# Two-layer sliding attention and feed-forward on one core: second products of a chunk's last group listed ahead of the next chunk's first ones, and weight forms made by ScalarE and GpSimd, six pairs per chunk

## The chip, the cores and the metric

The kernel runs on 1 core of one Trainium2 chip. The metric is the device time of one launch in microseconds (us), and the figure of a kernel is the median of its runs. Engines are named as in the profile: PE is TensorE, DVE is VectorE, ACT is ScalarE, POOL is GpSimd, SP is SyncE, which here only issues transfers.

## The reference

Two kinds of layer alternate, twice each, on 2048 rows of 576 numbers. The weights are shared between the two rounds.

```python
def _A_ref(x, wqkv, wo):                      # 32 heads of 18
    q, k, v = split(x @ wqkv)
    idx = pos[:, None] - 2 * arange(8)        # each row sees 8 rows, 2 apart, itself and back
    logits = (q . k[idx]) * 18 ** -0.5        # rows before the start are masked
    return (softmax(logits) . v[idx]) @ wo

def _B_ref(x, w1, w2):                        # 576 -> 4608 -> 576
    return silu(x @ w1) @ w2

x = x + _A_ref(layernorm(x), wqkv, wo)
x = x + _B_ref(layernorm(x), w1, w2)
x = x + _A_ref(layernorm(x), wqkv, wo)
x = x + _B_ref(layernorm(x), w1, w2)
```

All matrix products are made of float16 halves (a high and a low part of each operand, three products of halves in place of one), so that float32 accuracy is kept.

## The kernel before

**Chunks.** The rows are cut into 4 chunks of 512 (4 tiles of 128). With two rounds there are 8 chunk steps, s = 0 to 7; steps 0 to 3 are the first round, 4 to 7 the second. Chunk step s runs LayerNorm, the q/k/v products, attention on DVE, the projection by wo, LayerNorm, and the feed-forward. The attention part of step s+1 is worked on while PE does the feed-forward of step s, so PE nearly always has a product to make.

**Feed-forward.** Steps 0 and 1 use plain products (`ffn`). Steps 2 to 6 use `ffn_pairs`: the first products (w1) go by 18 pairs of 128-column blocks, each pair made by seven products P1 to P7 (a Strassen-Winograd scheme) of 7 matmuls each (line 1176). ACT copies partial sums out of PSUM (L1180), DVE adds to them (L1183), ACT applies silu (L1199, L1201, L1203), ACT makes the high half of h (L1206) and DVE the low half (L1209). The pairs form six groups of three. The second products of a group (w2, in `second`, line 1334) take h of its three pairs for each of four tiles j, 36 matmuls per tile, 144 per group; DVE adds the result into x (L894). Step 7 uses `ffn_twice`, whose second products follow a Strassen scheme too (lines 1237 and 1307).

**Forms.** Before the first products of a chunk, `forms` makes seven combinations of x on DVE (L1127, L1132), halves them on ACT (L1141, L1142) and DVE (L1146, L1147), and SP turns them by transposing transfers (L1151) into tile xb, which the matmuls of L1176 read. Nine such places exist, and a chunk holds seven, so most forms of a chunk are turned only as the last pair of the chunk ahead frees places.

**Weight forms.** Step 7 needs combinations of the w2 blocks. `prepare_second` makes them for 18 pairs q: SP loads two blocks (L1081, L1082), POOL makes four subtractions (L1088), ACT the high half with a scale (L1090), DVE the low half (L1092), POOL stores the result to DRAM (L1094, tile wts). Before, nine pairs are made after the attention of step 6 and nine after that of step 7, in two places of the area `kvs`, which the attention's keys and values use too; so the first two units of step 7's attention have a `hold` on `("wts", 8)`.

**Order.** Nothing is scheduled at run time. Each operation is declared with an engine, a planned duration and a priority (`op`), and a planner (`Plan.order`) writes one fixed instruction list per engine: at each moment of its own plan the ready operation of lowest priority number goes next. An operation that is late on the chip makes everything behind it on its engine wait. In step s the first products of pair q have priority s + 0.5 + 0.01 q; the q/k/v products, the attention and the projection of step s+1 have s, so they go first wherever they are ready. The second products of groups 0 to 4 have s + 0.5 + 0.01 (g+1) 3 and a little; those of the last group have s + 0.5 + SEAM with SEAM = 1, which is the priority of the next chunk's first products. "Seam" below means the stretch from the last pair of one chunk to the first pairs of the next.

Of the kernel before, what the change touches and what calls it, by code (L numbers as in the profile page):

```python
# [269 lines left out]
def sliding_attention_silu_ffn(ctx: ExitStack, tc: tile.TileContext, x, wqkv, wo, w1, w2, out):  # L270
# [230 lines left out]
    highs = []  # L501
    attended = []
    turned = []
# [237 lines left out]
    def attention(s, xT, wq, more=None):  # L741
# [4 lines left out]
        for u in range(NU):  # L746
# [12 lines left out]
            else:  # L759
                w = wq(u)  # L760
                hold = {S3: [("wts", NP // 2 - 1)], S3 + 1: [("wts", NP - 1)]}.get(s, []) if u < 2 else []
                if blk == 0:
                    def clear(kv=kv):
                        nc.gpsimd.memset(T(kv)[0:2, 0:3], 0.0)
                        nc.gpsimd.memset(T(kv)[0:1, 3:7], 0.0)
                    op("POOL", 1.86, clear, hold, [(kv, "edge")], pr_, after=free)
                else:
                    def edge(kv=kv, u=u):
                        a, b = T(kv)[0:2, 0:3], T(kv)[0:1, 3:7]
                        e = eds[lay, par, u]  # L770
# [298 lines left out]
    def prepare_second(q, prio, after):  # L1069

        b = Buf("v2")

        def rows6():
            return T(b)[:, 0:12 * KH].bitcast(F32).rearrange("p (a b) -> p a b", a=6)

        def split():
            return T(b)[:, 12 * KH:].rearrange("p (a b c) -> p a b c", a=4, b=2)

        def load():
            t = rows6()  # L1080
            nc.sync.dma_start(t[:, 0:2, :], w2[2 * q * P:(2 * q + 1) * P, :].rearrange("p (h c) -> p h c", h=2))  # L1081
            nc.sync.dma_start(t[:, 2:6:3, :], w2[(2 * q + 1) * P:(2 * q + 2) * P, :].rearrange("p (h c) -> p h c", h=2))  # L1082
        op("SP", 0.8, load, ["wsc"], [(b, 0)], prio, nbytes=P * 4 * KH * 4, after=after, lanes=2)

        def sums():
            t = rows6()
            for r, x, y in ((3, 1, 0), (1, 5, 1), (4, 5, 3), (2, 2, 4)):
                nc.gpsimd.tensor_tensor(t[:, r], t[:, x], t[:, y], op=ALU.subtract)  # L1088
        op("POOL", 3.4, sums, [(b, 0)], [(b, 0)], prio)
        op("ACT", 1.2, lambda: nc.scalar.activation(split()[:, :, 0, :], rows6()[:, 1:5], AF.Copy, scale=wst[:, q:q + 1]),  # L1090
           [(b, 0), "wsc"], [(b, 1)], prio)
        op("DVE", 1.4, lambda: nc.vector.scalar_tensor_tensor(split()[:, :, 1, :], rows6()[:, 1:5], wst[:, q:q + 1], split()[:, :, 0, :],  # L1092
                                                              op0=ALU.mult, op1=ALU.subtract), [(b, 0), (b, 1)], [(b, 1)], prio)
# [226 lines left out]
    def second(s, g, ng, hb, wbs, xs, d2):  # L1320
# [217 lines left out]
```

## Time and profile before

| what | value |
|---|---|
| runs of the kernel before | 2146.66, 2148.25, 2164.3 us; median 2148.25 us |
| profiled execution, its own time | 2152.83 us |
| its span, first to last instruction | 2151.0 us |
| PE busy in the span | 2106.6 us (98%) |
| DVE, ACT, POOL busy | 1709.5, 1010.5, 493.4 us |
| mean granted TensorE clock | 0.997 of full speed |

The profile shows one execution. Busy time of PE is the union of its matmuls, so span less busy time is the time in which no matmul ran. A window row gives for a stretch of the span the busy time and count of each engine, the granted TensorE clock (PEclk) and the share of the transfer engines. A wait row names the waiting engine, tile and line, then what released it, the total, the number of times and the longest. A chain row tells what the last-ending work hung on at that time.

### The profile page before, as it was taken

Reading aid. Unit: us, or ns where it says so; the run is one execution under the profiler, and the core shown is the slowest. Engines: PE = TensorE matmul, PEld = TensorE weight load, DVE = VectorE, ACT = ScalarE, POOL = GpSimd, SP = SyncE. Lnnn points to the kernel's source line nnn. Section 1 sums busy time; section 2 is a strip of 40 time slices with the busy share of each in tenths; the row PEclk is TensorE's granted clock in tenths of the full one; section 3 lists DMA queues with packets and bytes.
Section 4 is the critical chain, followed back from the end, with each engine's and each line's share of the span. In section 5 each row is a group of like instructions: output and inputs, shape, how many; then the busy total and the mean of one; then the engine's idle time right before and its main releaser. Section 6 shows DMA issues by size and latency. Waiting matters only on the chain.

```text
span 2151.0 us, 41793 instructions
## 1 busy us (share of the span) xinstructions
PE 2106.6 (98%) x16125; PEld 1567.9 (73%) x16125; DVE 1709.5 (79%) x2657; ACT 1010.5 (47%) x1839; POOL 493.4 (23%) x747
## 2 busy tenths in 40 slices
PE   8999999999999999999999999999999999999999
PEld 4556566655667888777886788867878867887887
DVE  8999999999978999689944999349995369964544
ACT  7555788654344553444243443344434434344443
POOL 2224656243332330011000100011031100233322
PEclk9999999999999999999999999999999999999999
DMA  6476777697889988875767667676688956679773
GB/s 181 153 227 248 248 262 262 168 281 244 227 198 291 325 256 219 197 215 162 185 173 181 200 194 181 155 192 205 202 245 216 279 148 184 182 232 281 235 209 114
DMA packets 360015, 460.16 MB, mean 214 GB/s; under 512 B 148216, under 2 KB 286820, under 8 KB 355848
## 3 DMA queue, kind: packets, MB, share of 16 engines
q1 hardware_dynamic: 316904, 316.49, 53.4%
q0 software_dynamic: 40896, 139.89, 20.3%
q8 instruction: 126, 2.06, 0.4%
q10 hardware_dynamic: 2016, 1.11, 0.2%
q14 instruction: 73, 0.60, 0.1%
HBM read 330.61 MB, written 78.29 MB: 190 GB/s over the span
## 4 chain that ended last, share of the span: by engine, by line
PE 81%; DMA 8%; DVE 6%; issue 2%; ACT 1%; POOL 1%; SPq 0%; ACTq 0%; DVEq 0%; POOLq 0%
PE acc L1334 22%; PE z L1176 11%; PE misc L1176 10%; PE z L710 8%; PE z L1376 6%; PE acc L1395 6%; PE misc L710 5%; PE acc L887 4%; PE acc L1307 4%; PE z L1237 2%; PE misc L1237 2%; DMA xb<-yh 2%; DMA w<-w2s 1%; DMA w<-wfs 1%; DMA wq<-in_B_w_dram 1%
## 5 line engine op out<-in xcount | busy, mean ns | idle before, releaser
L1334 PE MATMUL acc<-w,h 128*128 128x288 f16 x4320 | 558.0, 287 | 1.2 <-DVE x L894 1.2
L1334 PEld LDWEIGHTS <-h 128*128 128x128 f16 x4320 | 423.6, 98 | 105.3 <-issue 1.4
L1176 PEld LDWEIGHTS <-w 128*128 128x128 f16 x4410 | 432.4, 98 | 76.7 <-issue 15.9
L1176 PE MATMUL z<-xb,w 128*128 128x256 f16 x2261 | 289.2, 274 | 8.2 <-DMA xb<-yo 4.0
L1176 PE MATMUL misc<-xb,w 128*128 128x256 f16 x2149 | 275.2, 273 | 8.1 <-ACT wq L1180 4.3
L1395 PE MATMUL acc<-w,h 128*128 128x288 f16 x1728 | 215.6, 286 | 2.1 <-DMA w<-w2s 2.1
L710 PEld LDWEIGHTS <-xa 128*128 128x128 f16 x1344 | 131.0, 98 | 112.7 <-issue 2.1
L1395 PEld LDWEIGHTS <-h 128*128 128x128 f16 x1728 | 168.4, 98 | 46.5 <-issue 2.5
L894 DVE SCALAR_TENSOR_TENSOR x<-acc,d,x 128x576 f32<-128x576 f32 x160 | 129.4, 811 | 83.2 <-PE acc L1334 77.4
L846 DVE TENSOR_TENSOR prs<-kvs,pe 128x1152 f32<-128x1152 f32 x128 | 169.6, 1351 | 0.8
L813 DVE TENSOR_TENSOR prs<-qts,kvs 128x2304 f32<-128x2304 f32 x64 | 163.3, 2552 | 5.3 <-ACT qts L781 4.1
L817 DVE TENSOR_REDUCE lg<-prs 128x128 f32<-128x2304 f32 x64 | 163.0, 2547 | 1.0
L853 DVE TENSOR_TENSOR prs<-prs 128x1152 f32<-128x1152 f32 (+1 forms) x128 | 135.1, 1056 | 3.3
L793 POOL DMA_DIRECT2D kvs<-kvs x64 | 33.9, 537 | 448.4 <-ACT qts L781 423.2
L1376 PE MATMUL z<-xb,w 128*128 128x512 f16 x588 | 130.8, 383 | 5.1 <-ACT h L1378 1.9
L887 PE MATMUL acc<-wo,yo 128*128 128x288 f16 x896 | 113.4, 286 | 1.7 <-ACT yo L489 1.2
L710 PE MATMUL z<-wq,xa 128*128 128x432 f16 x602 | 114.7, 346 | 0.0
L710 PE MATMUL misc<-wq,xa 128*128 128x432 f16 x574 | 110.3, 346 | 2.7 <-ACT xa L489 1.3
L1376 PEld LDWEIGHTS <-w 128*128 128x128 f16 x588 | 57.8, 99 | 75.5 <-issue 4.3
L1088 POOL TENSOR_TENSOR kvs<-kvs 128x288 f32<-128x288 f32 x72 | 67.0, 941 | 180.5 <-DMA kvs<-in_B_w_dram 124.3
L887 PEld LDWEIGHTS <-yo 128*128 128x128 f16 x896 | 87.6, 98 | 25.0 <-ACT yo L489 1.4
L1237 PEld LDWEIGHTS <-w 128*128 128x128 f16 x882 | 86.1, 98 | 15.8 <-issue 2.7
(286 smaller groups left out, 3193.0 us busy)
## 6 DMA issues: line engine op xcount, KB each, us to landing
w<-wfs SPq DMA_DIRECT2D x756, 160.0 KB
w<-w2s SPq DMA_DIRECT2D x216, 288.0 KB
wq<-wqs SPq DMA_DIRECT2D x17, 1080.0 KB
kvs<-kd POOLq DMA_DIRECT2D x8, 1584.0 KB, 10.3
w<-w1s SPq DMA_DIRECT2D x36, 320.0 KB
wfs<-xa POOLq DMA_DIRECT2D x18, 640.0 KB, 4.6
w2s<-w POOLq DMA_DIRECT2D x36, 288.0 KB, 4.1
kvs<-in_B_w_dram SPq DMA_DIRECT2D x36, 288.0 KB
```

The lines of the kernel that those rows point to most:

```text
L710: nc.tensor.matmul(T(m)[:, :3 * UC], a, b, start=n == 0, stop=n == len(pl) - 1)
L813: nc.vector.tensor_tensor(T(pr), T(qt)[:, j:j + 2, None, :].to_broadcast([P, 2, W, UC]), win(T(kv), j, 2), op=ALU.mult)
L817: nc.vector.tensor_reduce(T(lg)[:, j:j + 2].rearrange("p a w h -> p (a w h)"), T(pr).rearrange("p a w (h d) -> p (a w h) d", d=DH), axis=A ...
L846: nc.vector.tensor_tensor(T(pr)[:, a].rearrange("p w (h d) -> p w h d", d=DH), v, T(pe)[:, j + a, :, :, None].to_broadcast([P, W, UH, DH]) ...
L853: nc.vector.tensor_tensor(t[:, :, 0:h, :], t[:, :, 0:h, :], t[:, :, h:2 * h, :], op=ALU.add)
L887: nc.tensor.matmul(T(acc)[:, h, 0:288], a, b[:, h * 288:(h + 1) * 288], start=n == 0, stop=n == len(pl) - 1)
L894: nc.vector.scalar_tensor_tensor(t, T(acc)[:, :, 0:288], d, t, op0=ALU.mult, op1=ALU.add)
L1176: nc.tensor.matmul(t, w[:, u, :], v[:, r, :], start=first and m == 0, stop=m == 6, skip_group_check=True)
L1237: nc.tensor.matmul(t, w[:, u, :], v[:, r, :], start=first and m == 0, stop=m == 6, skip_group_check=True)
L1334: nc.tensor.matmul(T(acc)[:, h, 0:288], T(hb[t])[:, a, f, j * P:(j + 1) * P], T(wbs[t][f])[:, h, w, :], start=t == 0 and f == 0 and m == 0 ...
L1376: nc.tensor.matmul(T(z), v, u, start=m == 0, stop=m == len(pl) - 1)
L1395: nc.tensor.matmul(T(acc)[:, h, 0:288], T(hb[q])[:, a, j * P:(j + 1) * P], T(wbs[q][0])[:, h, w, :], start=q == 0 and m == 0, stop=q == n ...
```

## The change

- `second`: with LATE = 8 the second products of the last group get s + 0.5 + 0.18 and a little, as the other groups do, in every step that uses `second` (2 to 6). The number of matmuls stays.
- `prepare_second`: ACT scales the two loaded blocks in place (L1089 of the changed kernel), POOL makes the four subtractions (L1094), ACT the high half (L1096), POOL the low half by one subtraction of 1152 numbers per partition (L1097), POOL stores (L1099). DVE has no part in it. The forms are in one place of area `xa` (16 KH, where the turned input of the q/k/v products stands too) in place of two of `kvs`.
- Six pairs each are declared after the last q/k/v product of steps 4, 5 and 6 (list `fed`). The `hold` of step 7 is gone.
- `load_wt` reads the products 5, 7, 4, 6 from the places in their new sequence.

```diff
+LATE = 8
+FORMS = {4: (0, 6), 5: (6, 12), 6: (12, 18)}
-    parts("v2", [(KV, 0), (KV, 10 * WB)], [20 * KH], F16)
+    part("v2", XA, 1, [16 * KH], F16)
-                hold = {S3: [("wts", NP // 2 - 1)], S3 + 1: [("wts", NP - 1)]}.get(s, []) if u < 2 else []
...
+                    if u == NU - 1 and j == NJ - 1:
+                        fed.append(done)
...
         def load():
-            t = rows6()
-            nc.sync.dma_start(t[:, 0:2, :], w2[2 * q * P:(2 * q + 1) * P, :].rearrange("p (h c) -> p h c", h=2))
-            nc.sync.dma_start(t[:, 2:6:3, :], w2[(2 * q + 1) * P:(2 * q + 2) * P, :].rearrange("p (h c) -> p h c", h=2))
+            for f in range(2):
+                nc.sync.dma_start(rows4()[:, f * D:(f + 1) * D], w2[(2 * q + f) * P:(2 * q + f + 1) * P, :])
         op("SP", 0.8, load, ["wsc"], [(b, 0)], prio, nbytes=P * 4 * KH * 4, after=after, lanes=2)
+        op("ACT", 1.2, lambda: nc.scalar.activation(rows4(), rows4(), AF.Copy, scale=wst[:, q:q + 1]), [(b, 0), "wsc"], [(b, 0)], prio)
         def sums():
-            for r, x, y in ((3, 1, 0), (1, 5, 1), (4, 5, 3), (2, 2, 4)):
+            for r, x, y in ((0, 1, 0), (1, 3, 1), (3, 3, 0), (2, 2, 3)):
                 nc.gpsimd.tensor_tensor(t[:, r], t[:, x], t[:, y], op=ALU.subtract)
-        op("POOL", 3.4, sums, [(b, 0)], [(b, 0)], prio)
-        op("ACT", 1.2, lambda: nc.scalar.activation(split()[:, :, 0, :], rows6()[:, 1:5], AF.Copy, scale=wst[:, q:q + 1]),
-           [(b, 0), "wsc"], [(b, 1)], prio)
-        op("DVE", 1.4, lambda: nc.vector.scalar_tensor_tensor(split()[:, :, 1, :], rows6()[:, 1:5], wst[:, q:q + 1], split()[:, :, 0, :],
-                                                              op0=ALU.mult, op1=ALU.subtract), [(b, 0), (b, 1)], [(b, 1)], prio)
+        op("POOL", 3.8, sums, [(b, 0)], [(b, 0)], prio)
+        op("ACT", 1.2, lambda: nc.scalar.activation(split()[:, :, 0, :], four(), AF.Copy), [(b, 0)], [(b, 1)], prio)
+        op("POOL", 3.1, lambda: nc.gpsimd.tensor_tensor(split()[:, :, 1, :], four(), split()[:, :, 0, :], op=ALU.subtract),
+           [(b, 0), (b, 1)], [(b, 1)], prio)
...
-                    at = (pp + 0.01 * (g + 1) * n if g + 1 < ng else pp + SEAM) + 0.01 * ((j * n + t) // 6) + 0.005
+                    at = (pp + 0.01 * (g + 1) * n if g + 1 < ng or s < LATE or (j * n + t) * 3 < 8 * n else pp + SEAM) + 0.01 * ((j * n + t) // 6) + 0.005
...
-        if s in (S3 - 2, S3 - 1):
-            for q in range(*((0, NP // 2), (NP // 2, NP))[s - S3 + 2]):
-                prepare_second(q, s + 0.9, attended[s + 1:s + 2])
+        if s + 1 in FORMS:
+            for q in range(*FORMS[s + 1]):
+                prepare_second(q, s + 0.9, fed[-1:] if s + 1 >= NC else [o for k, o in S.writer.items() if k == ("wfs", NP - 1, 1)])
```

**Place 1: DVE, end of step 4 and start of step 5.** In the kernel before, from the low half of h of the last pair of step 4 (L1209) on; L1146 and L1147 halve the forms of step 5, L1183 adds for its first pair, L894 adds a second product into x, L813 is the first operation of step 6's attention:

```order
L1209 SCALAR_TENSOR_TENSOR h<-wq,sh_279,h 128x1024
L1146 TENSOR_TENSOR yo<-o,yo 128x256
L1147 TENSOR_TENSOR yo<-o,yo 128x64
...
L1183 TENSOR_TENSOR h<-z_95,h 128x256
L1183 TENSOR_TENSOR h<-misc_97,h 128x256
...
L1209 SCALAR_TENSOR_TENSOR h<-h,sh_279 128x1024
L894 SCALAR_TENSOR_TENSOR x_73<-acc_98,d_282,x_73 128x576
L813 TENSOR_TENSOR prs<-qts,kvs 128x2304
```

The same place in the changed kernel, where L1214 is the low half of h, L1151 and L1152 the halving, L897 the add into x, L1188 the add of a first product and L816 the attention:

```order
L1214 SCALAR_TENSOR_TENSOR h<-wq,sh_279,h 128x1024
L1151 TENSOR_TENSOR yo<-o,yo 128x256
...
L897 SCALAR_TENSOR_TENSOR x_73<-acc_99,d_282,x_73 128x576
L1151 TENSOR_TENSOR yh<-o,yh 128x256
...
L897 SCALAR_TENSOR_TENSOR x_73<-acc_98,d_282,x_73 128x576
L897 SCALAR_TENSOR_TENSOR x_74<-acc_99,d_282,x_74 128x576
L897 SCALAR_TENSOR_TENSOR x_74<-acc_98,d_282,x_74 128x576
L1188 TENSOR_TENSOR h<-misc_96,h 128x256
...
L1214 SCALAR_TENSOR_TENSOR h<-h,sh_279 128x1024
L816 TENSOR_TENSOR prs<-qts,kvs 128x2304
```

All four adds of the last group now stand ahead of the first pair of step 5; before, all four stood behind it, the first ahead of the attention and three further on. PE's list says the same: before, six products of the next chunk's first pair (42 of its 49 matmuls) and the q/k/v products of a unit stand between the last pair and the bulk of the last group's second products; now the 144 second products follow the last pair at once (12 of them ahead of its seventh product), then the q/k/v products, then the next chunk.

**Place 2: POOL, step 3.** The weight forms in the changed kernel, where L765 and L766 clear rows for the next attention and L1419 stores x:

```order
L1094 TENSOR_TENSOR xa<-xa 128x288 x4
L1097 TENSOR_TENSOR xa<-xa 128x4x288
L1099 DMA wts_208<-xa 128x2304
L765 MEMSET kvs 2x864
L766 MEMSET kvs 1x1152
L1094 TENSOR_TENSOR xa<-xa 128x288 x4
L1097 TENSOR_TENSOR xa<-xa 128x4x288
L1099 DMA wts_209<-xa 128x2304
```

Before, no form stands in step 3. In the changed kernel's lists three pairs are made in step 3, three in step 4, five in step 5 and seven in step 6, from pair 6 of the step on; before, eight are made in step 5 from pair 10 on, one early in step 6, six from pair 13 of step 6 on, and three in step 7.

**Place 3: ACT, pair 6 to 8 of step 3 in the changed kernel.** L1185 copies first products out of PSUM, L1204, L1206 and L1208 are silu, L1211 the high half of h, L839 the attention's exp:

```order
L1206 ACTIVATE h<-h,accw 128x512
L1208 ACTIVATE h<-h,accw 128x256
L1089 ACTIVATE xa<-xa,accw 128x1152
L839 ACTIVATE pe_81<-lg_80 128x256
L1204 ACTIVATE h<-misc_97,accw 128x256
L1211 ACTIVATE h<-h,sh_279 128x1024
L1096 ACTIVATE xa<-xa 128x4x288
L1185 ACTIVATE wq<-misc_96 128x256
L1185 ACTIVATE wq<-z_95 128x256 x2
```

ACT, which empties PSUM for PE, now has two operations of each pair's forms in its list: L1089 needs the load, L1096 needs POOL's four subtractions. Before it had one (L1090), behind the subtractions.

More of the change, by code (lines that the diff above doesn't have):

```diff
@@ L501, in sliding_attention_silu_ffn @@
     highs = []
-    attended = []
+    attended, fed = [], []
     turned = []
@@ L765, in clear @@
                         nc.gpsimd.memset(T(kv)[0:1, 3:7], 0.0)
-                    op("POOL", 1.86, clear, hold, [(kv, "edge")], pr_, after=free)
+                    op("POOL", 1.86, clear, [], [(kv, "edge")], pr_, after=free)
                 else:
@@ L772, in edge @@
                         nc.sync.dma_start(b.rearrange("p a b c -> p (a b c)"), e[1:2, :])
-                    op("SP", 0.8, edge, [("eds", lay, par, u)] + hold, [(kv, "edge")], pr_, nbytes=20000, lanes=2, after=free)
+                    op("SP", 0.8, edge, [("eds", lay, par, u)], [(kv, "edge")], pr_, nbytes=20000, lanes=2, after=free)
                 for j in range(NJ):
@@ L782, in attention @@
                     for a, b in ((0, 6), (6, 12), (12, 14)) if s + u + j == 0 else ((0, 14),):
-                        op("PE", 2.56 * (b - a) / 14, lambda j=j, m=m, w=w, a=a, b=b: qkv_matmul(xT, w, j, m, a, b),
-                           [(xT, j)] + hold + [w.keys[5 * h + k] for k in range(a // 3, (b + 2) // 3) for h in range(2)],
+                        done = op("PE", 2.56 * (b - a) / 14, lambda j=j, m=m, w=w, a=a, b=b: qkv_matmul(xT, w, j, m, a, b),
+                           [(xT, j)] + [w.keys[5 * h + k] for k in range(a // 3, (b + 2) // 3) for h in range(2)],
                            [m, (kv, "hold")] if lay else [m], pr_, after=free)
+                    if u == NU - 1 and j == NJ - 1:
+                        fed.append(done)
                     op("ACT", 0.78, evac, [m, ("su", u)], [(kv, j), (qt, j)], pr_ - (0 if s else 9))
@@ L1071, in prepare_second, with rows4, four @@
         b = Buf("v2")
-        def rows6():
-            return T(b)[:, 0:12 * KH].bitcast(F32).rearrange("p (a b) -> p a b", a=6)
+        def rows4():
+            return T(b)[:, 0:8 * KH].bitcast(F32)
+        def four():
+            return rows4().rearrange("p (a b) -> p a b", a=4)
         def split():
-            return T(b)[:, 12 * KH:].rearrange("p (a b c) -> p a b c", a=4, b=2)
+            return T(b)[:, 8 * KH:].rearrange("p (a b c) -> p a b c", a=4, b=2)
         def load():
-            t = rows6()
-            nc.sync.dma_start(t[:, 0:2, :], w2[2 * q * P:(2 * q + 1) * P, :].rearrange("p (h c) -> p h c", h=2))
-            nc.sync.dma_start(t[:, 2:6:3, :], w2[(2 * q + 1) * P:(2 * q + 2) * P, :].rearrange("p (h c) -> p h c", h=2))
+            for f in range(2):
+                nc.sync.dma_start(rows4()[:, f * D:(f + 1) * D], w2[(2 * q + f) * P:(2 * q + f + 1) * P, :])
@@ L1083, in prepare_second @@
         op("SP", 0.8, load, ["wsc"], [(b, 0)], prio, nbytes=P * 4 * KH * 4, after=after, lanes=2)
+        op("ACT", 1.2, lambda: nc.scalar.activation(rows4(), rows4(), AF.Copy, scale=wst[:, q:q + 1]), [(b, 0), "wsc"], [(b, 0)], prio)
         def sums():
-            t = rows6()
-            for r, x, y in ((3, 1, 0), (1, 5, 1), (4, 5, 3), (2, 2, 4)):
+            t = four()
+            for r, x, y in ((0, 1, 0), (1, 3, 1), (3, 3, 0), (2, 2, 3)):
                 nc.gpsimd.tensor_tensor(t[:, r], t[:, x], t[:, y], op=ALU.subtract)
-        op("POOL", 3.4, sums, [(b, 0)], [(b, 0)], prio)
@@ L1096, in load_wt @@
+        op("ACT", 1.2, lambda: nc.scalar.activation(split()[:, :, 0, :], four(), AF.Copy), [(b, 0)], [(b, 1)], prio)
+        op("POOL", 3.1, lambda: nc.gpsimd.tensor_tensor(split()[:, :, 1, :], four(), split()[:, :, 0, :], op=ALU.subtract),
+           [(b, 0), (b, 1)], [(b, 1)], prio)
+        op("POOL", 0.57, lambda: nc.gpsimd.dma_start(wts[q], T(b)[:, 8 * KH:]), [(b, 1)], [("wts", q)], prio, nbytes=P * 4 * KH * 4)
     def load_wt(q, k, prio, kind="wt"):
@@ L1102, in load_wt @@
         if src is None:
-            i = {7: 0, 4: 1, 5: 2, 6: 3}[k]
+            i = {5: 0, 7: 1, 4: 2, 6: 3}[k]
             src = wts[q][:, i * n:(i + 1) * n]
```

1 line of the change is left out of this document (removed).

## The prediction

> **What bounds the kernel now.** I read the busy times first, then the windows by stage, then PE's waits, then the timeline and the chain at one seam.
>
> ```profile
> PE 2106.6 (98%) x16125; PEld 1567.9 (73%) x16125; DVE 1709.5 (79%) x2657; ACT 1010.5 (47%) x1839; POOL 493.4 (23%) x747
> ```
>
> PE is the bound, and the change takes no matmul away. The only thing to win or lose is PE's idle time, 2151.0 - 2106.6 = 44.4 us. The windows show where it lies (window, its us, PE busy, PEld, DVE, ACT, POOL, clock, transfers):
>
> ```profile
> 0.00:640.00 640.00, 622.06 (x4001) 380.18 (x4002) 599.24 (x996) 384.29 (x670) 248.37 (x400) 1.00 0.74 225
> 878.00:955.00 77.00, 75.03 (x556) 54.12 (x555) 53.52 (x70) 34.33 (x79) 12.07 (x21) 1.00 0.85 227
> 955.00:1137.00 182.00, 182.00 (x1531) 149.64 (x1530) 140.36 (x239) 68.26 (x128) 7.14 (x10) 1.00 0.64 173
> 1137.00:1213.00 76.00, 72.05 (x517) 50.94 (x516) 49.46 (x58) 29.05 (x65) 13.09 (x22) 0.98 0.76 206
> 1399.00:1475.00 76.00, 72.33 (x517) 51.05 (x515) 49.16 (x58) 29.80 (x65) 8.68 (x16) 0.98 0.77 209
> 1555.00:1610.00 55.00, 49.93 (x408) 40.59 (x407) 49.97 (x103) 19.05 (x30) 20.50 (x25) 0.97 0.89 244
> 1669.00:1755.00 86.00, 83.27 (x654) 63.67 (x652) 38.98 (x55) 36.53 (x75) 10.60 (x18) 1.00 0.79 222
> 1755.00:1929.00 174.00, 174.00 (x1432) 139.90 (x1430) 153.67 (x207) 72.40 (x132) 31.67 (x38) 1.00 0.69 197
> 1929.00:2010.00 81.00, 77.28 (x668) 64.97 (x667) 40.73 (x63) 39.52 (x75) 33.66 (x43) 1.00 0.92 269
> 2010.00:2151.00 141.00, 136.20 (x1168) 113.92 (x1166) 67.40 (x94) 53.82 (x92) 34.23 (x48) 1.00 0.59 172
> ```
>
> The first 640 us hold 17.9 us of idle, which the change does not touch: the two lists of PE are the same up to the end of step 2. The last window holds 4.8, mostly the store at the end. In reach are the seams of steps 2/3, 3/4, 4/5, 5/6 and 6/7 (1.97, 3.95, 3.67, 2.73 and 3.72 us) and the window at 1555, where step 6's projection meets the first weight forms (5.07): together 21.1 us. Two seams have a clock of 0.98 and the window at 1555 has 0.97, so matmuls ran slower behind the long stops: 2 x 76 x 0.02 + 55 x 0.03 = 4.7 us more. That is 26 us, or 1.2%, and a perfect change could win no more. Within one chunk PE does not stop at all (182.00 of 182.00).
>
> What PE waited for at the seams:
>
> ```profile
> PE z L1176 <- DMA xb<-yo: 4.0, 1, 4.0
> PE z L1176 <- DMA xb<-yh: 3.7, 1, 3.7
> PE misc L1176 <- DMA xb<-yh: 2.0, 1, 2.0
> ...
> 1152.09 0.22 DVE L1147 TENSOR_TENSOR yo<-kvs,yo 128x64 f16<-128x64 f32 x1
> 1153.59 3.41 SPq L1151 DMA_TRANSPOSE xb<-yo  x2
> 1154.92 8.07 DMA xb<-yo
> 1163.13 1.65 PE L1176 MATMUL z<-xb,w 128*128 128x256 f16 x7 [3.95 <-DMA xb<-yo]
> ```
>
> The last two turned forms of step 4 are issued from 1153.59; the chain shows 8.07 us until they are there, and the seventh product of the first pair waits 3.95 us for them.
>
> **The change, part by part.**
>
> **1. The last group's second products go first.** 144 matmuls now stand between the last pair and the next chunk. What they and the end of a pair cost:
>
> ```profile
> 1127.97 1.47 PE acc L1334 x12
> 1129.44 0.76 PE misc L1176 x7
> 1130.20 7.35 PE acc L1334 x60
> ...
> 1144.53 0.93 PE L1176 MATMUL z<-xb,w 128*128 128x256 f16 x7
> 1145.50 0.47 ACT L1199 ACTIVATE wq<-z,accw 128x256 f32<-128x256 f32 x1
> 1146.00 1.15 ACT L1206 ACTIVATE h<-wq,sh 128x1024 f16<-128x1024 f32 x1
> 1147.18 1.28 DVE L1209 SCALAR_TENSOR_TENSOR h<-wq,sh,h 128x1024 f16<-128x1024 f32 x1 [2.64 <-ACT h L1206]
> ```
>
> Twelve second products take 1.47 us, so 144 take 17.6. Before, 10.2 us of q/k/v products (one unit) and six products of 0.76 lay between the last pair and the wait. Now 17.6 us more lie there, against 8.07 of transfer, so the wait on turned forms goes, with 12 us to spare. Won: 1.97 + 3.95 + 3.67 = 9.6 us and 3.0 of clock.
>
> But the group's own h is now late. The last product of the last pair runs from 1144.53 for 0.76 us, to 1145.29; its h is whole at 1147.18 + 1.28 = 1148.46. Only the twelve matmuls of the middle pair stand between (1.47 us, to 1146.76), and nothing else is listed. PE waits 1148.46 - 1146.76 = 1.7 us. Before, the next chunk's first pair hid this. Bounds: 1.2 us, if the four matmuls that need only the high half go ahead (4 x 0.12), and 4, if the four halving operations that stand beside it on ACT and DVE get in its way. I take 1.7, five times: 8.5 us lost. It is too short to cost clock: the 2.0 us stop of the 2/3 seam left its window at 1.00.
>
> The other two seams were not bound by turned forms. At 5/6 the change also takes a weight form and the `hold` away; I take its 2.73 us as gone. At 6/7 the wait is among step 7's own loads and copies; I take 1.7 of 3.72 as gone.
>
> **2. Weight forms.** DVE loses 18 operations, ACT gains 18, POOL gains 18:
>
> ```profile
> L1092 DVE SCALAR_TENSOR_TENSOR kvs<-kvs,accw 128x1152 f16<-128x1152 f32 x18 | 26.0, 1443 | 5.3 <-ACT kvs L1090 5.0
> L1090 ACT ACTIVATE kvs<-kvs,accw 128x1152 f16<-128x1152 f32 x18 | 22.5, 1251 | 29.4 <-POOL kvs L1088 28.2 <-DMA prs<-wts 0.8 <-DVE nt L517 0.3
> L1088 POOL TENSOR_TENSOR kvs<-kvs 128x288 f32<-128x288 f32 x72 | 67.0, 941 | 180.5 <-DMA kvs<-in_B_w_dram 124.3 <-DVE yh L874 53.8
> ```
>
> None of these engines is the bound, so 26.0 us off DVE and 22.5 more on ACT (of 47% busy) are worth nothing as such. What counts is where they make the operations behind them late.
>
> Step 6's projection at 1555: DVE is busy 49.97 of 55 us there. Its part in the forms leaves, but three pairs still fall beside that projection. Of 5.07 us and 1.65 of clock I take 3.1 and 1.0 as won.
>
> ACT: L1090 waited 28.2 us on POOL in 18 pairs. The window at 1755 holds six of these and PE lost nothing; at 1555, five and at most 5.07. Now ACT waits twice per pair, once on a load that POOL used to wait for (124.3 us, harmless there). Behind ACT stand the copies that free PSUM for PE. Cost between 0 and twice 5.07: I take 5 us.
>
> POOL's new subtraction of 1152 numbers has no row. Four of 288 take 3.76 us by the mean; as one operation it can hardly be longer, and a single one of 288 (0.94) is below it; the work is the former's, so I take 3.2. A pair is then 3.76 + 3.2 = 7.0 us of POOL. It lies beside attention, where DVE is nearly full:
>
> ```profile
> 1142.00:1306.00 164.00, 160.05 (x1242) 121.87 (x1240) 134.94 (x161) 69.16 (x131) 17.57 (x29) 0.99 0.71 198
> DVE h L1209 <- ACT h L1206: 11.0, 2, 8.3
> DVE h L1183 <- ACT h L1180: 4.3, 1, 4.3
> ...
> 1567.20 2.56 DVE L474 SCALAR_TENSOR_TENSOR yh<-o,so,yh 128x512 f16<-128x512 f32 x2
> 1567.66 0.80 POOL L1088 TENSOR_TENSOR kvs<-kvs 128x288 f32<-128x288 f32 x1
> 1298.80 0.94 DVE L474 SCALAR_TENSOR_TENSOR yh<-o,so,yh 128x512 f16<-128x512 f32 x2
> ```
>
> The same two L474 operations took 0.94 us alone and 2.56 beside POOL's subtractions, so the two engines hold each other up. This has a rule on the page "SBUF — State Buffer" of the Trainium skill (section "Who interferes with whom"): an operation of VectorE with two inputs in SBUF and an operation of GpSimd that reads SBUF exclude each other for a whole instruction. The rows above agree with it; attention has not been seen beside POOL's arithmetic in this trace.
>
> The grouped rows of that window for DVE:
>
> ```profile
> L846 DVE TENSOR_TENSOR prs<-kvs,pe 128x1152 f32<-128x1152 f32 x16 | 21.2, 1351 | 0.1
> L813 DVE TENSOR_TENSOR prs<-qts,kvs 128x2304 f32<-128x2304 f32 x8 | 20.4, 2554 | 0.3
> L853 DVE TENSOR_TENSOR prs<-prs 128x1152 f32<-128x1152 f32 x8 | 10.8, 1354 | 0.1
> L1209 DVE SCALAR_TENSOR_TENSOR h<-wq,sh,h 128x1024 f16<-128x1024 f32 x7 | 8.9, 1277 | 2.6 <-ACT h L1206 2.6
> ```
>
> Like L474 they take two operands from SBUF; together 61.3 of DVE's 134.94 us, with the smaller ones of their kind about half. So two and a half pairs per attention cost 2.5 x 7.0 / 2 = 9 us of DVE in each of steps 3 to 6. Against this stand 8.3 + 4.3 us of DVE idle at the seam, which go with the wait on turned forms, and PE's list has the projections of steps 4 and 5 some two pairs later than before. I take 1 us of lateness per step, 4 in all; the ends are 0 and what rival B gives.
>
> SP: with one place, a load now waits until the pair ahead is stored, and loads of w1 blocks stand behind it. The store's time, from the rows of L1094:
>
> ```profile
> DMA to landing us min/median/max: 4.0/5.4/7.3
> ```
>
> The w1 loads have twelve places, 9 us of products and more with the second products between, which hides a block of up to 7.3 us; I take 0. What went beyond the 9 would be PE's one for one.
>
> **Sum.** Won: 9.6 + 3.0 + 2.7 + 1.7 + 4.1 = 21.1. Lost: 8.5 + 5 + 4 = 17.5. Net 3.6 us less: span 2147.4, own time 2152.83 - 3.6 = 2149.2. The profiled run was 4.6 above the median, 2148.25; off the median it gives **2144.7 us**. A change of under 1% (21.5 us) is about what a measurement of this kernel can't tell from none.
>
> **Rivals.**
>
> **A, the forecast:** the seam's wait on turned forms becomes a shorter wait on h; the forms cost about what they cost before. 0.60.
>
> **B, slower: POOL's subtractions and DVE's attention exclude each other.** If every POOL operation of 2.5 pairs delays DVE, attention ends 17.5 us later in steps 3 to 6; less the 12.6 of idle and none for the place of the projection, PE stops 5 us at each of four projections, 20 in place of 4. POOL's four subtractions wait in turn behind DVE operations of 1.35 to 2.55 us, L1096 on ACT waits for them, and the ACT term doubles, 5 to 10. Together 2144.7 + 16 + 5 = 2166; with one more microsecond at each of the 18 pairs from late copies, 2184. It decides from some 3 us of DVE delay per pair on. For it: L474 above. Against: at 1755 six pairs cost PE nothing. 0.22. The rule of the Trainium skill on the page "SBUF — State Buffer" ("Who interferes with whom") speaks for B: it would have the engine that starts second wait for the whole of the other's instruction.
>
> **C, clean:** no PE time for ACT's and DVE's part, and 1555 wholly won: 2144.7 - 5 - 4 - 2.6 = 2133. For it: windows without idle beside forms. Against: ACT's waits double. 0.10.
>
> **D, the move only trades:** h at the seam waits 4 us, five times, since the halving of forms crowds ACT and DVE: 2144.7 + 11.5 = 2156. 0.08. Then the listing does not do what it says, as the first products of the next chunk were the cover.
>
> **How the numbers follow.** A, C and D lie within 1% of 2148.25; so does about half of B. Faster by over 1% needs under 2126.8, which even C does not reach: 0.03. Slower by over 1% (over 2169.7) is the upper half of B: 0.10. Same: 0.87. The range goes from somewhat below C, 2130, to B's middle, 2167.
>
> **What would show it.** Right: no wait of L1181 (the new number of L1176) on turned forms at the seams; five waits of some 1.7 us of L1339 (second products) on h; clock 1.00 at the seams; PE idle past 878 us of about 20 us instead of 26. Wrong: waits of the projection's matmuls on DVE or transfers in steps 3 to 6, attention operations on DVE well over 2.55 and 1.35 us, waits of L1096 on POOL beyond 50 us in total, or a span that moved by more than 20 us.

## The result and the profile after

| kernel | runs | median us | lowest to highest |
|---|---|---|---|
| before | 9 | 2152.18 | 2146.66 to 2164.30 |
| after | 9 | 2169.12 | 2162.56 to 2182.73 |

The changed kernel is slower by 0.8%: ratio 1.0077, with a 95% interval of 1.0050 to 1.0105, some 17 us. The prediction had 2144.7 us and a range of 2130 to 2167. The profiled execution of after took 2171.7 us (span 2169.9, of which PE was busy for 2109.3). So PE's idle time rose from 44.4 to 60.6 us, and its busy time by 2.7.

The first view of after is its windows by stage (window, its us, PE busy, PEld, DVE, ACT, POOL, clock, share of the transfers, GB/s). The seams of steps 2/3, 3/4, 4/5 and 5/6 start at about 878, 1150, 1419 and 1683; behind each stands the chunk beside whose products the attention of the next chunk and the weight forms run.

```profile
878.00:955.00 77.00, 71.46 (x539) 53.19 (x537) 38.27 (x63) 31.29 (x72) 7.48 (x14) 0.98 0.90 228
955.00:1150.00 195.00, 189.25 (x1557) 151.99 (x1555) 163.79 (x249) 77.76 (x140) 35.87 (x34) 1.00 0.66 181
1150.00:1215.00 65.00, 60.83 (x463) 44.93 (x461) 29.34 (x43) 24.17 (x56) 9.22 (x16) 1.00 0.86 228
1215.00:1419.00 204.00, 200.13 (x1622) 160.16 (x1621) 167.09 (x255) 82.61 (x148) 32.00 (x32) 0.98 0.67 181
1419.00:1490.00 71.00, 68.92 (x530) 51.50 (x529) 34.52 (x50) 29.33 (x64) 6.42 (x12) 1.00 0.87 232
1490.00:1683.00 193.00, 189.28 (x1559) 152.29 (x1558) 163.09 (x246) 82.62 (x144) 40.47 (x38) 1.00 0.70 196
1683.00:1752.00 69.00, 67.04 (x515) 49.96 (x513) 33.19 (x48) 28.03 (x62) 6.41 (x12) 1.00 0.86 230
1752.00:1948.00 196.00, 190.75 (x1567) 152.94 (x1566) 155.00 (x206) 86.79 (x150) 55.18 (x50) 1.00 0.64 187
```

In before PE did not stop at all inside the chunk at 955 (182.00 of 182.00) nor in the one at 1755 (174.00 of 174.00). Now each of the four long windows has 3.7 to 5.8 us of idle: 5.75 + 3.87 + 3.72 + 5.25 = 18.6 us, all of it behind the first weight forms of the window. The four seam windows hold 5.54, 4.17, 2.08 and 1.96 us, where before had 1.97, 3.95, 3.67 and 2.73 in windows of much the same length, so in sum they won nothing.

The second view is the list of what PE waited for, in after (us in total, times, longest):

```profile
PE misc L1181 <- DVE wq L1188: 9.0, 7, 2.5
PE z L1181 <- DVE wq L1188: 8.5, 7, 2.9
PE misc L1181 <- DMA w<-wfs: 5.2, 4, 3.7
PE z L1181 <- DMA w<-wfs: 3.8, 2, 3.6
...
PE acc L1339 <- DVE h L1214: 1.2, 1, 1.2
PE misc L1181 <- DMA xb<-yh: 0.7, 1, 0.7
```

L1181 is the first products (L1176 in before), L1188 the adds of DVE into their partial sums (L1183), `w<-wfs` the loads of first-half weights, L1339 the second products and L1214 the low half of h. The three waits of 2.0 to 4.0 us on turned forms (`xb`) are down to one of 0.7. In their place stand two kinds that before had hardly at all: 17.5 us on DVE's adds (1.2 before) and 9.0 us on first-half weights. Of the five waits of 1.7 us on h at the seams there is none: the one of 1.2 us stands at 1045, inside a chunk.

What the adds wait for is seen in the timeline of after (start, us, engine, line, what), inside the chunk of step 3:

```profile
1058.81 4.79 DVE L849 TENSOR_TENSOR prs<-kvs,pe 128x1152 f32<-128x1152 f32 x2
1058.84 3.54 POOL L1097 TENSOR_TENSOR xa<-xa 128x1152 f16<-128x1152 f32 x1 [1.27 <-ACT xa L1096]
...
1063.63 2.15 DVE L856 TENSOR_TENSOR prs<-prs 128x1152 f32<-128x1152 f32 x2
...
1073.57 0.38 DVE L1188 TENSOR_TENSOR wq<-z,wq 128x256 f32<-128x256 f32 x1
1073.86 0.41 DVE L1188 TENSOR_TENSOR wq<-misc,wq 128x256 f32<-128x256 f32 x1
1074.00 1.25 PE L1181 MATMUL z<-xb,w 128*128 128x256 f16 x10 [2.91 <-DVE wq L1188]
```

Two multiplies of attention (L849, 1.35 us each alone) took 4.79 us, begun 0.03 us ahead of POOL's new low half (L1097, 2.40 us by its median, here 3.54). DVE has no gap from there to 1073.57, so all that stands behind them in its fixed list moves back, the adds at 1073.57 among it, and PE waits 2.91 us.

### The profile page after: what moved, and what is told of

Same layout as the page of the kernel before. It is cut to its first block, busy times and chain, and to the rows that moved or that the text cites. A ratio compares the mean times of both kernels' runs of the same rounds, so it can differ in the third digit from the quotient of the medians.

```text
span 2169.9 us, 41768 instructions
## 1 busy us (share of the span) xinstructions
PE 2109.3 (97%) x16125; PEld 1567.3 (72%) x16125; DVE 1704.2 (79%) x2639; ACT 1027.8 (47%) x1857; POOL 553.5 (26%) x765
## 4 chain that ended last, share of the span: by engine, by line
PE 59%; DVE 12%; DMA 6%; issue 2%; ACT 1%; POOL 1%; SPq 0%; DVEq 0%; ACTq 0%; POOLq 0%
PE acc L1339 18%; PE misc L1181 8%; PE z L1181 8%; PE misc L712 4%; PE acc L1312 4%; PE acc L890 3%; PE z L712 3%; PE acc L1400 3%; PE z L1381 3%; DMA w<-wfs 2%; DVE prs L849 2%; PE z L1242 2%; PE misc L1242 2%; DVE prs L856 1%; DMA w<-w2s 1%
## 5 line engine op out<-in xcount | busy, mean ns | idle before, releaser
L1339 PE MATMUL acc<-w,h 128*128 128x288 f16 x4320 | 557.0, 287 | 1.2 <-DVE h L1214 1.2
L1181 PEld LDWEIGHTS <-w 128*128 128x128 f16 x4410 | 431.9, 98 | 96.2 <-issue 27.9
L1339 PEld LDWEIGHTS <-h 128*128 128x128 f16 x4320 | 423.8, 98 | 105.6 <-DVE h L1214 1.5
L1181 PE MATMUL z<-xb,w 128*128 128x256 f16 x2268 | 288.5, 273 | 14.7 <-DVE wq L1188 8.5
L1181 PE MATMUL misc<-xb,w 128*128 128x256 f16 x2142 | 275.2, 274 | 17.6 <-DVE wq L1188 9.0
L897 DVE SCALAR_TENSOR_TENSOR x<-acc,d,x 128x576 f32<-128x576 f32 x160 | 129.4, 812 | 82.4 <-PE acc L1339 75.9
L816 DVE TENSOR_TENSOR prs<-qts,kvs 128x2304 f32<-128x2304 f32 x64 | 165.8, 2590 | 18.9 <-DMA kvs<-kvs 17.7
L849 DVE TENSOR_TENSOR prs<-kvs,pe 128x1152 f32<-128x1152 f32 x128 | 178.7, 1422 | 0.9
L820 DVE TENSOR_REDUCE lg<-prs 128x128 f32<-128x2304 f32 x64 | 163.0, 2547 | 0.9
L856 DVE TENSOR_TENSOR prs<-prs 128x1152 f32<-128x1152 f32 (+1 forms) x128 | 142.5, 1113 | 3.2
L1094 POOL TENSOR_TENSOR xa<-xa 128x288 f32<-128x288 f32 x72 | 75.2, 1045 | 186.4 <-ACT xa L1089 182.2
L712 PE MATMUL misc<-wq,xa 128*128 128x432 f16 x602 | 114.9, 346 | 2.7 <-ACT xa L491 1.3
L890 PE MATMUL acc<-wo,yo 128*128 128x288 f16 x896 | 113.7, 286 | 1.2 <-ACT yo L491 1.2
L712 PE MATMUL z<-wq,xa 128*128 128x432 f16 x574 | 109.4, 346 | 0.1
L890 PEld LDWEIGHTS <-yo 128*128 128x128 f16 x896 | 87.5, 98 | 24.4 <-ACT yo L491 1.4
```

Of the source, the lines that this page charges most:

```text
L712: nc.tensor.matmul(T(m)[:, :3 * UC], a, b, start=n == 0, stop=n == len(pl) - 1)
L816: nc.vector.tensor_tensor(T(pr), T(qt)[:, j:j + 2, None, :].to_broadcast([P, 2, W, UC]), win(T(kv), j, 2), op=ALU.mult)
L820: nc.vector.tensor_reduce(T(lg)[:, j:j + 2].rearrange("p a w h -> p (a w h)"), T(pr).rearrange("p a w (h d) -> p (a w h) d", d=DH), axis=A ...
L849: nc.vector.tensor_tensor(T(pr)[:, a].rearrange("p w (h d) -> p w h d", d=DH), v, T(pe)[:, j + a, :, :, None].to_broadcast([P, W, UH, DH]) ...
L856: nc.vector.tensor_tensor(t[:, :, 0:h, :], t[:, :, 0:h, :], t[:, :, h:2 * h, :], op=ALU.add)
L890: nc.tensor.matmul(T(acc)[:, h, 0:288], a, b[:, h * 288:(h + 1) * 288], start=n == 0, stop=n == len(pl) - 1)
```

## The experiments

All are compared with runs of the kernel before on the same chip (medians 2152.4 to 2153.5 us); where two experiments are set against each other, they may come from different chips. The theory was that POOL's arithmetic for the weight forms holds up attention on DVE and so the adds (rival B's mechanism at another place), while the new listing at the seams only trades one wait for another. Against it stood: that the listing costs the time (S), that ScalarE's waits in order do (R1), and that SP is held up by the single place (R2).

**e1_order_only: the listing alone, on the kernel before.**

```diff
+LATE = 8
...
-                    at = (pp + 0.01 * (g + 1) * n if g + 1 < ng else pp + SEAM) + 0.01 * ((j * n + t) // 6) + 0.005
+                    at = (pp + 0.01 * (g + 1) * n if g + 1 < ng or s < LATE or (j * n + t) * 3 < 8 * n else pp + SEAM) + 0.01 * ((j * n + t) // 6) + 0.005
```

> The kernel before with the new place of the last group's second products alone; the weight forms stay as before. Theory (the loss comes from the weight forms' POOL arithmetic, and the new place only trades the wait on the turned forms for waits on first-half weights and on a late halo): 2150 to 2156 us, ratio 1.000 to 1.002, with 3 to 4 us stalls of the first products behind each seam. Rival S (the new place itself costs most of the 17 us): 2162 or more. The recorded prediction's sum for this part alone (won 9.6 + 3.0 + 2.7 + 1.7, lost 8.5): about 2144.

Measured: 2162.02 us, 1.0051 (1.0031 to 1.0070), 9 us slower: more than the theory allowed and just at the bound of S; by the medians it is a little over half of the loss of 17. The waits of PE in its profile (of an execution that was 13 us above its median; L1238 are the first products of the last chunk, L1177 those of the others):

```profile
PE misc L1238 <- DMA w<-wfs: 7.9, 1, 7.9
PE misc L1177 <- DMA w<-wfs: 5.0, 3, 3.5
PE z L1177 <- DMA w<-wfs: 4.5, 2, 3.8
```

The seams traded as thought: 9.5 us on first-half weights for the 9.7 on turned forms. (A wait of 3.9 us on turned forms stands at 681 us, at the seam of steps 1/2, which the listing does not touch and where the profile of before has none.) The largest new stop is in the last chunk, 7.9 us for a load, where before had 1.8 us (`PE z L1237 <- DMA w<-wfs: 1.8, 1, 1.8`).

**e2_forms_only: the weight forms of the change, second products listed as before.**

```diff
-LATE = 8
+LATE = 0
-... or s < LATE or (j * n + t) * 3 < 8 * n else pp + SEAM)
+... or s < LATE or False else pp + SEAM)
```

> The changed kernel with the last group's second products listed where they were before; the new weight forms alone. Theory: almost the whole loss, 2162 to 2170 us, with the adds behind attention late in steps 4 to 6. Rival S (the new place costs it): 2150 to 2155. The recorded prediction's sum for this part alone (won 4.1, lost 9): about 2157.

Measured: 2174.50 us, 1.0108 (1.0082 to 1.0134): 22 us slower, above the range of the theory and a little more than both parts together. On these weight forms S falls: they carry the whole loss, and the new listing wins 5 us by the medians, a difference that the scatter of the runs does not tell from none.

**e3_low_on_dve: the change with the low half on VectorE.**

```diff
-        op("POOL", 3.1, lambda: nc.gpsimd.tensor_tensor(split()[:, :, 1, :], four(), split()[:, :, 0, :], op=ALU.subtract),
+        op("DVE", 1.4, lambda: nc.vector.tensor_tensor(split()[:, :, 1, :], four(), split()[:, :, 0, :], op=ALU.subtract),
```

> The changed kernel with the low halves of the weight forms subtracted by VectorE instead of GpSimd: GpSimd's arithmetic per pair falls from about 6.9 to 4.2 us, VectorE gains 1.4 us. Theory (attention's two-operand instructions wait out GpSimd's): the loss in steps 4 to 6 falls by a third to a half, 2160 to 2165 us. Rival R1 (ScalarE waits in order on the loads and on GpSimd's sums, and its PSUM copies come late): no change, 2167 to 2171, since the sums and ScalarE's two passes stay. Rival R2 (the one buffer holds SyncE): 2165 to 2170.

Measured: 2147.60 us, 0.9985 (0.9967 to 1.0002). Eighteen operations of 2.75 us moved off POOL, and DVE has 24.3 us more to do (1.35 each); the kernel is 21.5 us faster than the change, more than the theory asked for. ACT's waits for the forms, from this profile and then from that of after:

```profile
ACT xa L1096 <- POOL xa L1094: 24.8, 12, 4.7
ACT xa L1089 <- DMA xa<-in_B_w_dram: 14.8, 7, 5.7
```

```profile
ACT xa L1089 <- DMA xa<-in_B_w_dram: 20.7, 6, 6.5
ACT xa L1096 <- POOL xa L1094: 15.2, 8, 3.5
```

They sum to 39.6 us here and 35.9 in after. ACT waits as much as in after and the loss is gone, so R1 falls as the cause of the loss.

**e4_pool_writes_only: POOL fills the same places in place of subtracting.** The eighteen sets of subtractions are left out, so the last step works on false weights; the planned costs, the lists and ACT's work are those of the change.

```diff
-                nc.gpsimd.tensor_tensor(t[:, r], t[:, x], t[:, y], op=ALU.subtract)
+                nc.gpsimd.memset(rows4()[:, 0:3 * KH], 0.0)
...
+            for i in range(2):
+                nc.gpsimd.memset(split()[:, :, 1, :], 0.0)
```

> The changed kernel with GpSimd's subtractions left out and fills of the same places in their stead, so the output is not the reference's; the planned costs and so the lists stay the same. Theory: attention's instructions fall back toward their lone durations where the fills are shorter than the subtractions, and 10 to 15 us come back: 2154 to 2160 us. Rival R1: ScalarE's wait on the loads stays (about 20 us of it) and only its wait on GpSimd goes, 2162 to 2168. If the fills themselves exclude VectorE for as long, 2168.

Measured: 2143.17 us, 0.9954 (0.9934 to 0.9975), 26 us under the change, more than the theory's 10 to 15. First its POOL and attention rows, then those of after (busy us, mean ns):

```profile
L1094 POOL MEMSET xa<- 128x864 f32 x72 | 59.3, 823 | 209.0 <-ACT xa L1089 205.9
L1099 POOL MEMSET xa<- 128x1152 f16 x36 | 38.2, 1062 | 1.0
L849 DVE TENSOR_TENSOR prs<-kvs,pe 128x1152 f32<-128x1152 f32 x128 | 169.8, 1352 | 0.9
L820 DVE TENSOR_REDUCE lg<-prs 128x128 f32<-128x2304 f32 x64 | 163.1, 2548 | 0.9
L856 DVE TENSOR_TENSOR prs<-prs 128x1152 f32<-128x1152 f32 x64 | 86.7, 1354 | 1.0
```

```profile
L1094 POOL TENSOR_TENSOR xa<-xa 128x288 f32<-128x288 f32 x72 | 75.2, 1045 | 186.4 <-ACT xa L1089 182.2
L1097 POOL TENSOR_TENSOR xa<-xa 128x1152 f16<-128x1152 f32 x18 | 49.4, 2747 | 32.5 <-ACT xa L1096 32.5
L849 DVE TENSOR_TENSOR prs<-kvs,pe 128x1152 f32<-128x1152 f32 x128 | 178.7, 1422 | 0.9
L820 DVE TENSOR_REDUCE lg<-prs 128x128 f32<-128x2304 f32 x64 | 163.0, 2547 | 0.9
L856 DVE TENSOR_TENSOR prs<-prs 128x1152 f32<-128x1152 f32 x64 | 91.0, 1421 | 1.0
```

POOL is still busy for 97.5 of 124.6 us, but it reads nothing, and the multiplies are back at 1.35 us. The long windows of this kernel:

```profile
955.00:1150.00 195.00, 195.00 (x1615) 157.70 (x1614) 156.43 (x256) 82.24 (x156) 26.61 (x35) 1.00 0.71 191
1215.00:1400.00 185.00, 185.00 (x1535) 149.72 (x1532) 150.54 (x242) 76.85 (x141) 24.74 (x33) 1.00 0.71 194
1490.00:1683.00 193.00, 193.00 (x1612) 157.24 (x1610) 143.57 (x247) 81.21 (x150) 33.61 (x43) 1.00 0.79 213
1752.00:1928.00 176.00, 176.00 (x1481) 144.48 (x1480) 126.21 (x195) 81.33 (x148) 43.73 (x53) 1.00 0.69 198
```

No idle at all in them, against 18.6 us, with the same lists but for the fills. The fills are also 27 us shorter in total than the subtractions, and ACT's waits for the forms are 19.6 us here, so the 26 us are not the price of POOL's reading alone; e3, where ACT's waits stayed, is the narrower test. The operation with one operand from SBUF, the reduction L820, is the same in both (2.55 us).

**e5_low_in_four: the low half on GpSimd as four short subtractions.**

```diff
-        op("POOL", 3.1, lambda: nc.gpsimd.tensor_tensor(split()[:, :, 1, :], four(), split()[:, :, 0, :], op=ALU.subtract),
...
+            for i in range(4):
+                nc.gpsimd.tensor_tensor(split()[:, i, 1, :], four()[:, i], split()[:, i, 0, :], op=ALU.subtract)
...
```

> The changed kernel with GpSimd's low-half subtraction (128x1152, 2.40 us) issued as four of 128x288; the planned cost and all lists stay, and GpSimd's total work is not less. Theory, by length: a VectorE instruction waits out at most the one GpSimd instruction that runs, so with four short ones most of the loss goes, as it did with the low half on VectorE: 2148 to 2157 us, and attention's 1.35 us multiply (1.42 on average in the changed kernel) falls to about 1.37. Rival, by total: GpSimd's whole arithmetic time is what is taken from VectorE: 2165 to 2172 us, 1.42 stays.

Measured: 2170.40 us (2155.31 to 2174.46), 1.0072 (1.0043 to 1.0100): no gain clear of the scatter, and far from the 2148 to 2157 us that the theory by length asked for. It falls, and the rival by total stands. The profile is of one of its two fastest runs (2159.2 us). L849 in it, then in after (shortest/median/longest):

```profile
L849 DVE TENSOR_TENSOR prs<-kvs,pe x128: 1339/1351/1949, 72.0 to 1840.5; 128x1152 f32<-128x1152 f32 x128
```

```profile
L849 DVE TENSOR_TENSOR prs<-kvs,pe x128: 1339/1352/3528, 71.3 to 1852.5; 128x1152 f32<-128x1152 f32 x128
```

The longest single hold-up shrinks from 2.18 to 0.60 us, as one short subtraction for one long would make it, but there are more of them. Over the five attention operations with two operands in SBUF (L816, L849, both sizes of L856, L857), mean less lone mean times count gives 20 us in after, 16 in this profile (of a run 11 us under the median), 7 in e3 and 0 in e4.

**e8_old_seam_low_on_dve: the fourth corner, undisturbed forms and the old listing.** (e3 with the two lines of e2.)

> The kernel with the low half on VectorE and the old place of all the last group's second products: the fourth corner, which with the kernel that has the new order and low half on VectorE (2147.6) prices the new order with weight forms that do not disturb. Theory (the new order trades one wait for another): 2145 to 2151 us. If the order alone costs as on the kernel before (9 us there): 2138. If it gains as on the disturbed forms (5 us there): 2153 or more.

Measured: 2154.95 us, 1.0010 (0.9995 to 1.0026). With forms that disturb little, the new listing is worth 2154.95 - 2147.60 = 7.4 us: a gain, and this one is clear of the scatter. The theory had 2151 at most here; "only trades" falls for these forms.

**e6_partial: e3, with only two thirds of the last group's second products ahead.** The line of `second` already holds that rule; with LATE = 0 it applies in every step.

```diff
-LATE = 8
+LATE = 0
```

> The kernel with the low half on VectorE, and of the last group's second products only the first two thirds ahead of the next chunk's first products, the last third between these. Theory (behind the new seam the first products alone outrun the first-half weights, as the waits on their transfers show, 7.7 us in the kernel with the low half on VectorE): the late third covers these transfers, 2138 to 2145 us. Rival (the transfers are late because the DMA engines are full there, and a third more or less does not matter): 2145 to 2150. Rival O (the old order's wait on turned forms comes back): 2150 or more.

Measured: 2138.32 us, 0.9931 (0.9914 to 0.9948), 9 us below e3. The place of the 3/4 seam in after, by the windows, PE's longest wait and the chain there:

```profile
1183.00:1240.00 57.00, 52.83 (x382) 37.91 (x381) 41.10 (x41) 23.94 (x47) 7.15 (x12) 0.97 0.66 193
```

```profile
1200.98 0.78 PE z L1181 x7
1201.76 0.02 issue
1201.77 12.79 DMA w<-wfs
1214.56 0.04 issue
1214.61 0.50 PE misc L1181 x3
```

A load of first-half weights is issued when a first product frees its place at 1201.76, and arrives 12.79 us later; by then PE has run through the other places and stood 3.7 us. With that stop the mean clock of the window is 0.97, and from 1215 to 1240, behind it, 0.93. The same stretch in e6:

```profile
1160.00:1235.00 75.00, 73.77 (x555) 54.04 (x554) 53.19 (x57) 32.57 (x63) 10.90 (x19) 1.00 0.72 215
```

There 1.2 us of idle are left, none of it on a load, and the clock is 1.00: the last third of the second products gives the loads time, and the first two thirds still cover the turned forms (one wait of 1.4 us on these is left in e6's whole profile).

**e9_partial_old_forms and e10_partial_new_forms: the two-thirds place with the other weight forms.** (e1 and the change, each with LATE = 0.)

> The kernel before, weight forms and all, with two thirds of the last group's second products ahead of the next chunk's first products and the last third between them. Theory (the two-thirds place takes both waits of the seam, on the turned forms and on the first-half weights, whatever the weight forms): 2142 to 2150 us, some 10 to 18 below the kernel with all of them ahead (2162). Rival (before's weight forms, in the last chunks and in the halo's buffers, do not go with any earlier place): 2155 or more.

> The changed kernel, its weight forms on ScalarE and GpSimd as they are, with the two-thirds place. Theory (the place is worth some 9 us and GpSimd's subtractions cost some 20, apart from each other): 2156 to 2164 us. Rival (the disturbed attention mattered only because the first products were bunched): 2140 to 2148.

Measured: 2152.25 us, 0.9994 (0.9981 to 1.0006), and 2156.92 us, 1.0027 (1.0012 to 1.0043). The place is worth 10 and 12 us against all of them ahead, and 9 with e3's forms, so it is worth much the same on all. For e10 the theory holds; e9 came out 2 us above its range, since it started from 2162 and won only the least that was expected. e10 stands 19 us above e6, so GpSimd's low half costs as much beside that place. In e9's profile the last chunk keeps the stop of e1: 6.4 us in place of 7.9.

**e11_sums_on_dve: e6 with the four sums of each pair on VectorE too.**

```diff
-                nc.gpsimd.tensor_tensor(t[:, r], t[:, x], t[:, y], op=ALU.subtract)
-        op("POOL", 3.8, sums, [(b, 0)], [(b, 0)], prio)
+                nc.vector.tensor_tensor(t[:, r], t[:, x], t[:, y], op=ALU.subtract)
+        op("DVE", 1.8, sums, [(b, 0)], [(b, 0)], prio)
```

> The kernel with the two-thirds place and the low half on VectorE, and the four sums of each pair on VectorE too, so that GpSimd does no arithmetic for the weight forms. The attention instructions stand 8 us longer in all beside GpSimd's sums in the profile of 2139.9 us; on VectorE the 72 sums would take about 32 (estimate from its 128x288 subtraction of 0.45 us). Theory (what counts is VectorE's time in these steps): slower, 2140 to 2150 us. Rival (only the order matters in which VectorE comes to the adds, and a lock's wait is worse than work that the plan knows): 2130 to 2137.

Measured: 2133.91 us, 0.9902 (0.9886 to 0.9918), faster than both kernels of the case by 18.5 and 35 us. The theory (VectorE's time in these steps counts) falls and the rival's range holds: the sums take 32.8 us of DVE, and the kernel is 4.4 us faster than e6.

```profile
L1094 DVE TENSOR_TENSOR xa<-xa 128x288 f32<-128x288 f32 x72 | 32.8, 455 | 7.0 <-ACT xa L1089 5.1
L849 DVE TENSOR_TENSOR prs<-kvs,pe 128x1152 f32<-128x1152 f32 x128 | 170.2, 1351 | 0.6
```

All medians together (us; rows the place of the last group's second products, columns the weight forms):

| | as before | as changed | low half on VectorE | all on VectorE |
|---|---|---|---|---|
| behind the next first products (before) | 2152.8 | 2174.5 | 2155.0 | not run |
| all ahead of them (change) | 2162.0 | 2169.1 | 2147.6 | not run |
| two thirds ahead | 2152.3 | 2156.9 | 2138.3 | 2133.9 |

## Why the prediction was wrong

**What held.** PE is the bound, and nearly all of the change is its idle time. The wait on turned forms went, as worked out. POOL's work for a pair came out as forecast: 6.9 us (124.6 over 18 pairs) against 7.0. Rival B, given 0.22, had the exclusion of the two engines right. That its 2166 us is near the 2169 measured is luck, since it came by another path: B let PE stop at four projections and doubled the ACT term, and neither showed.

**By parts.** The weight forms were forecast to cost 9 us and win 4.1, 4.9 net, and cost 22 (e2). The listing was forecast to win 8.5 and won 5 (e2 less after). The two misses, 17 and 3.5 us, make up the 20.5 us between the forecast change of -3.6 and the 17 measured.

**The step that failed: "I take 1 us of lateness per step, 4 in all", and with it the 5 us for ACT.** Nine microseconds stood for the weight forms' effect on PE. The runs put it at 21.5 us for the low half alone (after less e3), 1.2 us per pair, and at 23 to 26 for all of GpSimd's subtractions (e10 less e11 with the two-thirds place; after less e4). The nearest row was in the text, L474 with 0.94 us alone and 2.56 beside POOL's subtractions; the text made of it 9 us of DVE in each of four steps, some 35 in all, more than the 20 us by which attention was in fact longer. What failed is the step from there to PE: the 9 us were set off against 12.6 us of DVE idle at the seam and a later projection. Both covers were in the wrong place. The projection never waited on attention (`PE acc L890 <- ACT yo L491: 1.2`, as before): the operations late were the adds L1188, which stand in DVE's list between attention's operations all through the chunk, and for which PE waits within the same pair. Idle at a seam does not help them.

The argument against B, that at 1755 six pairs cost PE nothing, failed as evidence: before made its forms where no attention was running. Half of its POOL subtractions lie between 1559 and 1716 us, behind the attention of step 6, and half from 1863 on, behind that of step 7; none stands beside the attention operations, whose longest multiply is therefore 1.36 us (shortest/median/longest):

```profile
L846 DVE TENSOR_TENSOR prs<-kvs,pe x128: 1339/1351/1359, 72.3 to 1855.2; 128x1152 f32<-128x1152 f32 x128
L1088 POOL TENSOR_TENSOR kvs<-kvs x72: 784/794/1982, 1559.0 to 1991.9; 128x288 f32<-128x288 f32 x72
```

It was the move into the time of attention that let the two engines meet. Even the four sums alone, which before has too, lengthen attention there: by 7 us in e3, against 20 with the new subtraction.

The rule of the Trainium skill cited for B (page "SBUF — State Buffer", section "Who interferes with whom") says that a VectorE instruction with two SBUF inputs contends with a GpSimd instruction that reads SBUF, and not with one that only writes it. The runs agree: up to 3.53 us for 1.35 beside the 2.40 us subtraction, up to 1.95 beside the short ones, 1.36 at most beside fills of 0.82 and 1.06 (e4's longest), and the one-input reduction L820 unmoved at 2.55.

**"ACT: Cost between 0 and twice 5.07: I take 5 us".** ACT's waits for loads and sums did come, 35.9 us of them, but with 39.6 of them e3 is 21.5 us faster. PE's waits on ACT's copies (L1185) come to 4.2 us in after, as the 4.3 in before, though elsewhere: 2.8 of them stand in the window at 1752, one of 1.17 us right behind a wait of 6.46 us of L1089 on its load. So 5 us was too much, but not nothing. The sign named for B, waits of L1096 beyond 50 us, was therefore the wrong one to watch (15.2); the one beside it, attention well over 1.35 us, was right.

**"Only the twelve matmuls of the middle pair stand between".** The rows were read at a place where the second products stand in twelves. At the seam the second tile's products of the two earlier pairs were ready too, and after ran all of them in one piece:

```profile
1154.33 1.63 PE L1339 MATMUL acc<-w,h 128*128 128x288 f16 x12
1155.80 0.93 PE L1181 MATMUL z<-xb,w 128*128 128x256 f16 x7
1156.56 16.33 PE L1339 MATMUL acc<-w,h 128*128 128x288 f16 x132
1172.73 2.72 PE L712 MATMUL z<-wq,xa 128*128 128x432 f16 x14
```

The first add into x (L897) starts at 1162.65, when some 60 of the 144 have run (estimate from the 16.33 us of the 132), and not after a tile's 36: the second tile's 24 went in between, while h was made ready. None of the 8.5 us for h was paid at a seam.

**"The w1 loads have twelve places, 9 us of products ... I take 0".** What went beyond it was PE's one for one, as the text said, but it was taken as nothing. With no second products between them the first products use up their places faster than the loads arrive (12.79 us at the 3/4 seam, with the transfers at 0.86 to 0.90 in the seam windows), and 9.0 us of waits came, with the clock lost behind them. So part 1 came out near its size on the new forms (8.5 us won by its sum; 5, within the scatter, by e2 and after, and 7 by e8 and e3) with a wrong term in it: the loss is to the weights and not to h.

**"Step 6's projection: 3.1 and 1.0 won".** The window of that step kept 3.72 us of idle in after, for the reason of the other three; in e4 it has none. The gain was there for the taking and was given back.

**"About what a measurement of this kernel can't tell from none".** The measured interval, 1.0050 to 1.0105, tells 0.8% from none.

**What stays open.** On the weight forms of before, the new listing costs 9 us, where it gains some 5 to 7 on the others. The profiles of e1 and e9 place 6 to 8 us in one stop of the last chunk's first products for a load, where the change and the kernels with its places for the forms show 3.4 or less. In e1 and e9 weight forms are still being made in that chunk, and in the change they are done before it, but before has them there too and stops for 1.8; why the listing makes it long was not tried. In e1's profile the window from 1948 to the end has 17.3 us of idle and a clock of 0.96, against 8.5 us and 1.00 in the last 222 us of before; that execution lay 13 us above the median of its kernel, so how much of the 9 us lies there stays open too. That SP is held up by the single place (R2) has no test of its own; its loads of the weight blocks waited in after only on PE's q/k/v products, for the start that `fed` sets or for the area `xa`, which these products read.

## What to carry to other kernels

Before work goes to GpSimd because it is idle, look at what VectorE runs at the same time. Here its two-operand instructions took 20 us longer beside GpSimd's subtractions, cutting one of these in four did not help, and 57 us more work on VectorE was cheaper than 125 us on GpSimd. Price such a delay at the next instruction in the same list that the bounding engine waits for, not at the end of the stage. And where a filler is moved ahead, ask what else it covered: here the second products hid the weight loads, and leaving a third of them where they were was better than either extreme on the new weight forms, and as good as the old place on those of before.

## What the runs showed that was not expected

- Fills on GpSimd of 0.82 us (128x864 f32) and 1.06 us (128x1152 f16) did not lengthen VectorE's two-operand instructions at all: 1.360 us at most, 1.351 by the median.
- The same subtraction takes 2.40 us on GpSimd and 1.35 on VectorE at 128x1152, 0.80 and 0.455 at 128x288, alone.
- A single stop of PE of 3.7 us left its 57 us window with a granted clock of 0.97; the window at 955, with 5.75 us of idle in three stops of 1.2 to 2.9, had 1.00, as had the 75 us of e6 with 1.2 us of idle.
